# A re-laid first batch and a GpSimd broadcast for the second batch's softmax reciprocals, in a low-rank attention and gated FFN kernel

## The chip, the cores and the metric

One core of a Trainium2 chip runs the whole kernel. The metric is the device time of one execution, in microseconds (us), as the median of several; the span of a profiled execution is some 1.8 us shorter than its time. Runs of two kernels are compared when they alternate on the same chip.

## The reference, cut to what matters

```python
k_proj = np.einsum('ks,bhsd->bhkd', E, k)        # 8 batches, 8 heads, 1024 positions, 64 wide; k_proj has 64 rows
v_proj = np.einsum('ks,bhsd->bhkd', F, v)
scores = scale * np.matmul(q, k_proj.transpose(0, 1, 3, 2))
attn = np.exp(scores - max); attn = attn / (sum(attn) + 1e-09)
x = np.matmul(attn, v_proj)                      # then (8192, 512)
gate = 1.0 / (1.0 + np.exp(-(x @ w_gate)))       # w_gate, w_val: 512 x 1536
out = (gate * (x @ w_val)) @ w_out               # w_out: 1536 x 512
```

Nearly all the arithmetic is the FFN. Attention is a side chain of small steps, one batch ahead of it.

## The kernel before

The FFN of a batch is two blocks of 512 rows. A block is twelve m-steps (eight matmuls of 128x512, 1.73 us), four output projections of 2.7 us, and between them the next batch's attention is put at numbered places ("spots"). Batches, halves of a batch and blocks are counted from 0. Batch 0 has no FFN to hide behind: its first half is the start-up.

```python
# start-up (cut); busy(n) is n dummy matmuls of 128x128 that keep TensorE going
busy(40)
for R in range(2):                        # K, four heads at a time
    project(0, 0, [bk, bk], 0, R); busy(4); keep_k(bk, 0, R); turn_k(whole, R); busy(8)
qt(0, ("DVE", "ACT")); busy(6)            # Q transposed into one PSUM bank, copied out by two engines
sc(0); qt(1, ("DVE", "DVE")); busy(6)     # scores, exp
den(0); sc(1); busy(4)                    # row sums, reciprocal, split into two bf16 halves (rhi, rhl)
bc(0); den(1); v_part(0, whole); busy(4)  # broadcast of the reciprocals by matmuls; V
bc(1); xo(0); busy(8)                     # attention output, scaled: xT
v_part(1, att)
# ... the FFN's first pair of m-steps, with xo(1) between

# batch 1 (b == 1), one step per spot (cut)
def kv():  project K and V into one bank; keep_k; keep_v by four ScalarE copies
def den(): row sums of all eight heads, then four reciprocals of 128x128 on VectorE
def split(): two more VectorE instructions make rhl
def bc(rnd): four matmuls broadcast rhl, four ScalarE copies make rb
spots = (16, 17, 18, 19, 20, 20, 22, 23, 24, 25)   # kv, turn, sc, sc, den, split, bc, bc, xo, xo

# batches 2 to 7 in place of split and bc
def gather():  four SyncE DMAs of 8 KB bring one row per head into rrow
def spread(rnd): eight GpSimd broadcasts of 512 columns make rb
```

The softmax here doesn't subtract the row's maximum and nothing guards it: scores larger than these inputs give would overflow.

## Time and profile before

| | before |
|---|---|
| time, median of 3 at first | 576.91 us (576.17 to 576.95) |
| the execution of the profile | 575.25 us, span 573.4, mean clock 1.0 |
| TensorE busy | 97% of the span |
| first FFN matmul | 25.85 us |
| waits of TensorE in the first 93 us | 1.06, 0.93 and 1.02 in the start-up, 1.17 at block 1, 1.82 for rhl in batch 1 |

The row of the page that shows TensorE's busy share in 40 slices of 14.3 us, in tenths:

```profile
PE   5799989999999999999999999999999999999997
```

Apart from the last slice, all that is below 9 lies in the first six, so I looked at the first 90 us.

### The profile page before, as it was taken

To read this page: it belongs to the slowest core of one execution; us is meant where nothing else is said; L and a number is where in the kernel's file an instruction comes from. 1 tells how busy PE (TensorE), PEld (TensorE's weight loads), DVE (VectorE), ACT (ScalarE), POOL (GpSimd) and SP (SyncE) were. 2 spreads that over 40 slices of the span, in tenths; PEclk is the share of its full clock that TensorE was granted. 3 is DMA by queue.
4 is the path that set the end of the run, shared out by engine and by line. 5 is a ranking of instruction groups with operands and counts; after the bars stand their busy time and mean duration, and the time that the engine had idled before them with its cause. 6 is when DMAs were issued, how large, how long until landed. Compare 5 with 4: busy or idle time off the path is not lost.

```text
span 573.4 us, 7766 instructions
## 1 busy us (share of the span) xinstructions
PE 556.9 (97%) x3060; PEld 248.8 (43%) x3060; DVE 251.5 (44%) x403; ACT 176.2 (31%) x310; POOL 107.2 (19%) x148
## 2 busy tenths in 40 slices
PE   5799989999999999999999999999999999999997
PEld 5443434444444444444444444444444444444443
DVE  3546356325633546335453264434463354633332
ACT  2444561342224322333223422144223332222220
POOL 9400200104400071001800035000610007000000
PEclk9999999999999999999999999999999999999999
DMA  9999896955656159430796046670501101010012
GB/s 159 199 201 186 144 204 159 173 112 104 113 117 102 37 113 153 86 84 22 123 170 116 23 85 107 138 105 37 113 19 46 38 20 39 37 38 21 35 38 91
DMA packets 76421, 56.02 MB, mean 98 GB/s; under 512 B 34688, under 2 KB 67968, under 8 KB 76384
## 3 DMA queue, kind: packets, MB, share of 16 engines
q0 software_dynamic: 33984, 29.89, 34.4%
q1 hardware_dynamic: 42400, 25.63, 17.6%
q8 instruction: 24, 0.39, 0.3%
q14 instruction: 13, 0.11, 0.1%
HBM read 60.29 MB, written 16.78 MB: 134 GB/s over the span
## 4 chain that ended last, share of the span: by engine, by line
PE 95%; DVE 3%; ACT 1%; issue 0%; DVEq 0%
PE pF L210 86%; PE pA L210 9%; ACT eT L214 1%; DVE rden L769 1%; DVE xT L639 0%; DVE rden L583 0%; DVE count L327 0%; DVE hT L910 0%; DVE dsel L388 0%; ACT sig L214 0%; DVE rhl L780 0%; DVE rhl L594 0%; DVE ost L937 0%; ACT qT L214 0%; ACT kp L214 0%
## 5 line engine op out<-in xcount | busy, mean ns | idle before, releaser
L910 DVE SCALAR_TENSOR_TENSOR hT<-sig,pF 128x512 bf16<-128x512 f32 x192 | 130.7, 685 | 200.5 <-PE pF L210 153.1
L214 ACT ACTIVATE sig<-pF 128x512 f32<-128x512 f32 x192 | 114.3, 599 | 317.6 <-PE pF L210 315.2
L210 PE MATMUL pF<-xT,wG 128*128 128x512 bf16 x768 | 198.3, 379 | 1.8 <-DVE xT L639 1.8
L210 PE MATMUL pF<-xT,wV 128*128 128x512 bf16 x768 | 197.7, 379 | 0.0
L210 PE MATMUL pF<-wO,hT 128*128 128x512 bf16 x732 | 168.1, 379 | 0.0
L210 PEld LDWEIGHTS pF<-xT,wV 128*128 128x128 bf16 x768 | 75.2, 98 | 90.3
L210 PEld LDWEIGHTS pF<-xT,wG 128*128 128x128 bf16 x768 | 72.2, 98 | 96.6 <-issue 12.9
L815 POOL PARTITION_BROADCAST rb<-rrow x96 | 70.7, 798 | 217.1 <-DMA rrow<-rden 212.0
L210 PEld LDWEIGHTS pF<-wO,hT 128*128 128x128 bf16 x732 | 70.4, 98 | 88.7 <-issue 6.2
L937 DVE TENSOR_SCALAR ost<-pF 128x512 f32<-128x512 f32 x61 | 42.2, 692 | 97.8 <-PE pF L210 95.5
L214 ACT ACTIVATE eT<-pA 128x512 bf16<-128x512 f32 x62 | 32.2, 606 | 9.5 <-PE pA L210 9.5
L840 DVE TENSOR_TENSOR xT<-pA,rb 128x512 bf16<-128x512 f32 x56 | 34.7, 682 | 0.0
L228 POOL DMA_DIRECT2D KV<-in_v_dram x9 | 7.8, 871 | 87.3 <-PE pF L210 84.9
L769 DVE RECIPROCAL rden<-pA 128x128 f32<-128x128 f32 x28 | 23.7, 909 | 0.0
L210 PE MATMUL pA<-KV,EFT 128*64 128x512 bf16 (+2 forms) x176 | 15.4, 319 | 1.0 <-DVE xT L639 1.0
L214 ACT ACTIVATE kpd<-pA 64x1024 bf16<-64x1024 f32 x6 | 6.1, 1017 | 28.3 <-PE pA L210 28.3
L228 POOL DMA_DIRECT2D KV<-in_k_dram x9 | 8.0, 890 | 33.3 <-PE pF L210 33.2
L210 PEld LDWEIGHTS pA<-KV,EFT 128*64 128x64 bf16 x176 | 8.0, 109 | 8.0 <-issue 4.1
L210 PE MATMUL pA<-qT,kpD 64*64 64x512 bf16 (+1 forms) x136 | 10.2, 370 | 0.5 <-ACT qT L214 0.3
L210 PE MATMUL pA<-eT,vpD 64*64 64x512 bf16 (+1 forms) x140 | 10.4, 367 | 0.0
L214 ACT ACTIVATE vpD<-pA 64x512 bf16<-64x512 f32 (+2 forms) x20 | 9.7, 484 | 2.2 <-PE pA L210 1.8
L228 POOL DMA_DIRECT2D Qb<-in_q_dram x11 | 9.4, 866 | 0.0
(70 smaller groups left out, 109.3 us busy)
## 6 DMA issues: line engine op xcount, KB each, us to landing
out_dram<-ost SPq DMA_DIRECT2D x64, 256.0 KB, 2.0
Qb<-in_q_dram POOLq DMA_DIRECT2D x7, 1024.0 KB, 15.9
KV<-in_k_dram POOLq DMA_DIRECT2D x7, 1024.0 KB, 10.8
KV<-in_v_dram POOLq DMA_DIRECT2D x7, 1024.0 KB, 11.4
wO<-in_moe_w_out_dram POOLq DMA_DIRECT2D x1, 1536.0 KB, 13.0
wG<-in_moe_w_gate_dram POOLq DMA_DIRECT2D x5, 256.0 KB, 19.7
wV<-in_moe_w_val_dram POOLq DMA_DIRECT2D x5, 256.0 KB, 20.2
KV<-in_k_dram POOLq DMA_DIRECT2D x2, 512.0 KB, 8.9
```

The source lines that it names most:

```text
L210: return add("PE", lambda e: e.matmul(o, lhsT, rhs, **kw), r=r, x=[("bank", b)])
L214: return add("ACT", lambda e: e.activation(o, i, func, scale=scale), r=r, w=w, x=x)
L228: add("POOL", lambda e: e.dma_start(o, i), r=r, w=w, dma=sem)
L769: lambda e, cc=cc: e.reciprocal(rden[:, cc], bank[bk][:, cc]),
L815: lambda e, n=n, i=2 * rnd + c, j=j, parts=parts: e.partition_broadcast(rb[0:parts, n, :], rrow[32 * j : 32 * j + 1, i, :], channels=parts),
L840: lambda e, r=r, g=g, n=n, bk=bks[g]: e.tensor_tensor(xT[s][:, r, :, 256 * g : 256 * g + 256], bank[bk][:, :].rearrange("p (f c) -> p f c" ...
L910: lambda e: e.scalar_tensor_tensor(hT[blk % 2][:, m, :], sg[:, :], 1.0, bank[pv][:, :], ALU.add, ALU.mult,),
L937: lambda e: e.tensor_scalar(o[:, :], bank[pb][:, :], 0.5, None, op0=ALU.mult),
```

## The change

It has two parts. In batch 0 it drops dummies, gives each copy of the first Q half a bank of its own, puts the scores of the second half of heads ahead of the first half's row sums, and names every PSUM bank by hand. In batch 1 it projects K and V at different places, starts three m-steps earlier, and takes the reciprocals' way of the later batches: four gathers and sixteen GpSimd broadcasts in place of split, eight matmuls and eight ScalarE copies.

```diff
-        whole, ffn, att = Ring(AB + FB[:3]), Ring(FB), Ring(AB)
+        whole = Ring((A0, A1) + (A2, A3, F0, F1) + (A0, A1) + (F2, A2) + ...)   # cut, 26 turns by hand
+        ffn, att = Ring(FB), Ring(AB)
@@ qt: one bank per copy
-                bk = ring.next()
                 for rr, eng in enumerate(engines):
+                    bk = ring.next()
@@ start-up
-        busy(40)
+        busy(20)
...
-            busy(8)
+            busy(10 if R == 0 else 4)
...
+        sc(1)
         den(0)
-        sc(1)
-        busy(4)
+        busy(10)
+        den(1)
         bc(0)
-        den(1)
-        v_part(0, whole)
-        busy(4)
+        v_part(0)()
+        busy(6)
         bc(1)
         xo(0)
-        busy(8)
+        busy(4)
+        keep = v_part(1)
+        keep()
@@ batch 1
-                kv, turn_kd, sc(0), sc(1), den, split, bc(0), bc(1), xo(0), xo(1)          (cut)
-                spots = (16, 17, 18, 19, 20, 20, 22, 23, 24, 25)
+                k_alone, turn_k, v_alone, sc(0), sc(1), den, gather, spread(0), spread(1), xo(0), xo(1)
+                spots = (13, 14, 16, 16, 17, 18, 18, 18, 18, 24, 25)
```

The last four output projections also take their banks from another ring.

More of the change, by code (lines that the diff above doesn't have):

```diff
@@ L153, in bass_linformer_attn__then__ffn_glu_sigmoid_kernel @@
         dsel8 = sbuf("dsel8", [P, 2, 4, 32], BF16)
-        bsel = sbuf("bsel", [P, 2, 2, 64], BF16)
         bsel8 = sbuf("bsel8", [P, 4, 2, 64], BF16)
@@ L198, in next @@
                 return b
-        whole, ffn, att = Ring(AB + FB[:3]), Ring(FB), Ring(AB)
+        A0, A1, A2, A3 = AB
+        F0, F1, F2, F3 = FB
+        whole = Ring(
+            (A0, A1)
+            + (A2, A3, F0, F1)
+            + (A0, A1)
+            + (F2, A2)
+            + (A3, A3)
+            + (F0, F1)
+            + (A0, A1)
+            + (A2, A0)
+            + (A3, F0)
+            + (F1, F2)
+            + (A1, A2)
+            + (A3, A0)
+            + (A1, A2)
+        )
+        ffn, att = Ring(FB), Ring(AB)
         def mm(b, o, lhsT, rhs, r, start=True, stop=True, tp=None, tr=False):
@@ L398, in constants @@
                         )
-            for t, k, m, i, v in ((bsel8, "bsel8", 8, 1, 0.5), (bsel, "bsel", 4, 2, 0.25)):
+            for t, k, m, i, v in ((bsel8, "bsel8", 8, 1, 0.5),):
                 dve(
@@ L518, in qt @@
             def qt(R, engines):
-                bk = ring.next()
-                ob = bank[bk][:, :].bitcast(BF16)
-                for x in range(4):
-                    for t in range(2):
-                        c = x * 2 + t
-                        mm(
-                            bk,
-                            ob[:, c * P : (c + 1) * P],
-                            Qb[s][:, 4 * R + x, (2 * hf + t) * P : (2 * hf + t + 1) * P],
-                            ident[:, :],
-                            [("Q", s, hf, R), "ident"],
-                            tr=True,
-                        )
-                o = qv[:, R, :, 256 * hf : 256 * hf + 256]
-                i = ob[:, :].rearrange("p (x c) -> p x c", x=4)
-                for rr, eng in enumerate(engines):
-                    oo, ii = (a[:, 2 * rr : 2 * rr + 2, :] for a in (o, i))
+                for rr, eng in enumerate(engines):
+                    bk = ring.next()
+                    ob = bank[bk][:, :].bitcast(BF16)
+                    for x in range(2):
+                        for t in range(2):
+                            c = x * 2 + t
+                            mm(
+                                bk,
+                                ob[:, c * P : (c + 1) * P],
+                                Qb[s][:, 4 * R + 2 * rr + x, (2 * hf + t) * P : (2 * hf + t + 1) * P],
+                                ident[:, :],
+                                [("Q", s, hf, R), "ident"],
+                                tr=True,
+                            )
+                    o = qv[:, R, 2 * rr : 2 * rr + 2, 256 * hf : 256 * hf + 256]
+                    i = ob[:, 0:512].rearrange("p (x c) -> p x c", x=2)
                     ws = [("qT", s, hf, R, rr)]
                     if eng == "ACT":
-                        act(oo, ii, [], ws, b=bk)
+                        act(o, i, [], ws, b=bk)
                     else:
-                        dve(lambda e, oo=oo, ii=ii: e.tensor_copy(oo, ii), [], ws, b=bk)
+                        dve(lambda e, o=o, i=i: e.tensor_copy(o, i), [], ws, b=bk)
             def sc(R):
@@ L670, in kv @@
                 bk = att.next()
-                if b == 1:
-                    project(2 * b % 3, 0, [bk, bk], 0)
-                    project((2 * b + 1) % 3, 1, [bk, bk], 256)
-                    keep_k(bk, 0)
-                    keep_v([bk, bk], 256, ["ACT"] * 4)
-                    return
                 for t in range(NT):
@@ L708, in kv, with k_alone, v_alone @@
                     )
+            def k_alone():
+                bk = att.next()
+                project(2 * b % 3, 0, [bk, bk], 0)
+                keep_k(bk, 0)
+            def v_alone():
+                bk = att.next()
+                project((2 * b + 1) % 3, 1, [bk, bk], 0)
+                keep_v([bk, bk], 0, ["ACT"] * 4)
             def turn_kd():
-                if b == 1:
-                    turn_k(att)
-                    return
                 add(
@@ L773, in den @@
                     )
-            def split():
-                rd = [("rden", c, R) for c in range(4) for R in range(2)]
-                ri = [("rhi", R) for R in range(2)]
-                dve(lambda e: e.tensor_copy(rhi[:, :], rden[:, :]), rd, ri)
-                dve(
-                    lambda e: e.scalar_tensor_tensor(
-                        rhl[:, :], rhi[:, :], rows[:, 3, 0:1], rden[:, :], ALU.mult, ALU.add
-                    ),
-                    rd + ri + ["rows"],
-                    [("rhl", R) for R in range(2)],
-                )
-            def bc(rnd):
-                for j in range(4):
-                    n, bk, jj = 4 * rnd + j, att.next(), slice(32 * j, 32 * j + 32)
-                    mm(
-                        bk,
-                        bank[bk][:, :],
-                        bsel[jj, rnd, :, :].rearrange("p h d -> p (h d)"),
-                        rhl[jj, :],
-                        ["bsel", ("rhl", j // 2)],
-                        tp=(32 * j, 0),
-                    )
-                    act(rb[:, n, :], bank[bk][:, :], [], [("rb", n)], b=bk)
             def gather():
@@ L849, in xo @@
                         )
+            if b == 1:
+                return [
+                    k_alone,
+                    lambda: turn_k(att),
+                    v_alone,
+                    lambda: sc(0),
+                    lambda: sc(1),
+                    den,
+                    gather,
+                    lambda: spread(0),
+                    lambda: spread(1),
+                    lambda: xo(0),
+                    lambda: xo(1),
+                ]
             return [
@@ L856, in attention @@
                 den,
-                split if b == 1 else gather,
-                (lambda: bc(0)) if b == 1 else (lambda: spread(0)),
-                (lambda: bc(1)) if b == 1 else (lambda: spread(1)),
+                gather,
+                lambda: spread(0),
+                lambda: spread(1),
                 lambda: xo(0),
@@ L961, in bass_linformer_attn__then__ffn_glu_sigmoid_kernel, with v_part @@
             turn_k(whole, R)
-            busy(8)
+            busy(10 if R == 0 else 4)
+        def v_part(R):
+            bks = [whole.next(), whole.next()]
+            project(1, 1, bks, 0, R)
+            return lambda: keep_v(bks, 0, ["ACT", "DVE", "ACT", "DVE"], R)
         qt(0, ("DVE", "ACT"))
@@ L967, in bass_linformer_attn__then__ffn_glu_sigmoid_kernel @@
         busy(6)
+        sc(1)
         den(0)
-        sc(1)
-        busy(4)
-        def v_part(R, ring):
-            bks = [ring.next(), ring.next()]
-            project(1, 1, bks, 0, R)
-            keep_v(bks, 0, ["ACT", "DVE", "ACT", "DVE"], R)
+        busy(10)
+        den(1)
         bc(0)
-        den(1)
-        v_part(0, whole)
-        busy(4)
+        v_part(0)()
+        busy(6)
         bc(1)
         xo(0)
-        busy(8)
-        for _ in range(-att.turn % 4):
-            att.next()
-        v_part(1, att)
-        start_xo = half_unit(0, att)[4]
+        busy(4)
+        keep = v_part(1)
+        keep()
         load_q(1)
@@ L1018, in bass_linformer_attn__then__ffn_glu_sigmoid_kernel @@
                     if len(m) == 2:
-                        todo.append(lambda: first_pair(lambda: start_xo(1)))
+                        todo.append(lambda: first_pair(lambda: xo(1)))
                     else:
@@ L1030, in bass_linformer_attn__then__ffn_glu_sigmoid_kernel @@
             if b == 0:
-                qt, sc, den, bc, xo = half_unit(1, att)
-                put(5, lambda: (qt(0, ("DVE", "ACT")), qt(1, ("DVE", "ACT"))))
-                put(6, lambda: sc(0))
-                put(7, lambda: (den(0), sc(1)))
-                put(8, lambda: (den(1), bc(0)))
-                put(9, lambda: (xo(0), bc(1)))
-                put(10, lambda: xo(1))
-                spots = (16, 17, 18, 19, 20, 20, 22, 23, 24, 25)
+                qt2, sc2, den2, bc2, xo2 = half_unit(1, att)
+                put(5, lambda: (qt2(0, ("DVE", "ACT")), qt2(1, ("DVE", "ACT"))))
+                put(6, lambda: sc2(0))
+                put(7, lambda: (den2(0), sc2(1)))
+                put(8, lambda: (den2(1), bc2(0)))
+                put(9, lambda: (xo2(0), bc2(1)))
+                put(10, lambda: xo2(1))
+                spots = (13, 14, 16, 16, 17, 18, 18, 18, 18, 24, 25)
             else:
@@ L1062, in bass_linformer_attn__then__ffn_glu_sigmoid_kernel @@
         for tt in range(4):
-            oproj(last, tt, whole.next())
+            oproj(last, tt, ffn.next())
         plan.emit(nc, es, final=[f"out{i}" for i in range(4)])
```

## The prediction

> **What bounds the kernel now.** I read the page first (busy shares, then the chain that ended last), then TensorE in order of time with the idle time before each group, then the other engines around each gap, then the DMA issues with their time to landing. The page:
>
> ```profile
> PE 556.9 (97%) x3060; PEld 248.8 (43%) x3060; DVE 251.5 (44%) x403; ACT 176.2 (31%) x310; POOL 107.2 (19%) x148
> ...
> PE 95%; DVE 3%; ACT 1%; issue 0%; DVEq 0%
> ```
>
> TensorE is busy 97% of 573.4 us and carries 95% of the chain. A table of busy time by stretch gives TensorE 67.0 of the 67 us from 93 to 160, so what is saved before 93 us should pass to the end undiminished, and nothing else can pay. So only the first 93 us matter: start-up, one gap in batch 0, and the attention of batch 1 (batches, halves and blocks are counted from 0; a block's FFN is twelve m-steps of eight matmuls, 1.73 us each). TensorE in order of time (start, length, group, idle before it):
>
> ```profile
> 5.54 1.94 PE L210 MATMUL pA<-identf,EF 128*128 128x128 f32 x8 [5.54 <-DVE dsel L388]
> 7.28 3.76 PE L210 MATMUL pF<-ident 128*128 128x128 bf16 x40
> 10.97 0.64 PE L210 MATMUL pA<-KV,EFT 128*64 128x128 bf16 x16
> ...
> 20.11 0.22 PE L210 MATMUL pF<-rhl,bsel 32*128 32x128 bf16 x1 [1.06 <-DVE rhl L594]
> ...
> 25.28 0.64 PE L210 MATMUL pA<-KV,EFT 128*64 128x128 bf16 x16 [1.02 <-DVE xT L639]
> 25.85 0.39 PE L210 MATMUL pF<-xT,wG 128*128 128x512 bf16 x1
> ...
> 53.71 0.60 PE L210 MATMUL pF<-xT,wG 128*128 128x512 bf16 x2 [1.17 <-DVE xT L639]
> ...
> 80.46 0.40 PE L210 MATMUL pA<-rhl,bsel 32*128 32x512 bf16 x4 [1.82 <-DVE rhl L780]
> ```
>
> See the 40 dummy matmuls (pF<-ident) that only bridge to the first K data; the FFN's first matmul at 25.85; and the 1.82 us wait for the reciprocals' split in batch 1.
>
> **What the Trainium skill says.**
> - "TensorE: Matmul & The Clock Gate", Part 1, The HAM clock gate: the array runs at half clock until about 3.4 us of activity. The trace agrees: the 40 dummies start (3.76-0.22)/39 = 91 ns apart, eight later ones (0.62 us in all) 57 ns. With the page's 107 and 56 ns the switch is near 10.1 us, an estimate.
> - "Perfetto Trace Analysis", Matmuls: independent groups should rotate through PSUM banks so that eviction hides. The trace agrees: the Q transposes of one bank have two readers, and ScalarE idles 1.03 us before its copy, until VectorE's is done.
> - "DMA: Bandwidth & Descriptors", Queues, rings and completion order: a DMA engine alternates between its queues by packets, so a small transfer waits beside big loads. The trace agrees: an output store landed in 2.0 us at the median, in 4.8 when issued at 84.31, while loads ran.
> - "SBUF — State Buffer", Who interferes with whom: a VectorE instruction with one SBUF input doesn't contend with GpSimd outside its two-port modes. hT (one SBUF, one PSUM input) took 0.69 us during batch 2's broadcasts and before them.
>
> **Part 1, start-up.** The change drops 18 of 92 dummies, splits each Q-transposing bank, puts the scores of the second half of heads ahead of the first half's denominators, and lays banks out. Issue start plus time to landing gives the arrivals, which don't move: K halves 1.34+8.0 = 9.3 and 2.23+9.8 = 12.0; Q 13.4 and 14.7; V 18.4 and 20.9; first weights 21.5 to 23.7. Walking the new order with the old durations:
> - 20 dummies at 107 ns end near 9.5 instead of 11.0. K half 0 projects there, partly cold, done by 10.5. K half 1 then waits for data: 12.1 instead of 12.88, so 0.8 us saved, not 1.5.
> - The old chain from there to the transposed K is 1.36 us; four dummies instead of eight follow. Q transposes start near 13.7 (was 14.69). VectorE copies bank one from 14.05 (0.42) while ScalarE copies bank two from 14.3 (0.60), no longer in series. Scores end near 15.3 (was 16.75): 1.5 saved.
> - The second Q half puts both copies in one bank, so its second transposes wait for the first copy; its scores end near 17.2 (was 18.7). Denominators, 0.95+0.28+0.34 us of VectorE each, come 0.4 later behind the scores; the two chains run back to back on VectorE and end near 20.9 (was 22.6). V's two copies (0.62) end near 21.5, output matmuls start there (was 23.30), and xT lands 1.84 us later, near 23.4 (was 25.14).
> - V half 1 (landed 20.9) now projects while xT is written, where it used to cost 0.57 after it. FFN starts near 23.45.
>
> Saving 25.85-23.45 = **2.4 us**. Weights don't stop it: the tightest chunk, the fourth, lands at 33.0 (gate) and 34.3 (value), wanted at 37.45 and 38.32 less 2.4. The 1.17 us gap at 53.71 stays: its matmuls and VectorE chain are untouched.
>
> **Part 2, batch 1.** Other rows used:
>
> ```profile
> 66.03 1.57 ACT L214 ACTIVATE vpD<-pA 64x256 bf16<-64x256 f32 x4
> ...
> 75.77 3.38 DVE L769 RECIPROCAL rden<-pA 128x128 f32<-128x128 f32 x4
> 79.19 0.43 DVE L778 CAST rhi<-rden 128x512 bf16<-128x512 f32 x1
> 79.65 0.75 DVE L780 SCALAR_TENSOR_TENSOR rhl<-rhi,rows,rden 128x512 bf16<-128x512 bf16 x1
> ```
>
> GpSimd in batch 2, whose way batch 1 now takes (SyncE issued its four gathers from 133.29):
>
> ```profile
> 135.72 0.79 POOL L815 PARTITION_BROADCAST rb<-rrow  x1 [31.45 <-DMA rrow<-rden]
> 136.68 6.09 POOL L815 PARTITION_BROADCAST rb<-rrow  x8 [0.16 <-DVE ost L937]
> 142.93 5.43 POOL L815 PARTITION_BROADCAST rb<-rrow  x7 [0.16 <-POOL rb L815]
> ```
>
> Gone: eight broadcasting matmuls, two groups of 0.33 us, 0.66 on the path; the 1.82 us gap; eight ScalarE copies (4.1 us) and split's 1.2 us of VectorE, off the path. K and V matmuls stay at 32 (1.87 us). Gain 2.5 us. New costs on TensorE:
> - **V's bank.** V is projected directly before the scores. After K, its transpose and V, the scores' four banks end on V's own. V's four ScalarE copies take 1.57+0.1 us; TensorE has 0.35 us of score matmuls ahead of that bank. Wait 1.35 us.
> - **hT behind the reciprocals.** Four reciprocals (3.38 us) start about 0.9 after the denominators and delay the next hT to 5.0 after them. Four m-steps now follow without an output projection between; the third one's value matmuls want that hT's bank at 2.5x1.73 = 4.3. Wait 0.7 us.
> - **Broadcasts.** From first gather to the first eight broadcasts done is about 8.7 us, to all sixteen 15.1. Gathers start 4.3 us after the denominators, so rb is complete at 19.4 and the last xT 0.69 later, 20.1. TensorE's way from the denominators to block 2: four m-steps 6.92, the wait of 0.7, four projections 10.8, outputs 1.12, and 0.65 of block 2's own first matmuls, 20.2. With batch 2's latency it just fits; I count 0.05 us. But then the DMA engines were idle; here gathers go out near 74.5, when W_out and three 1 MB loads are under way (issued from 60.17, the last landing at 65.54+23.1 = 88.6). The store of 84.31, which met the same loads (the page's median is 2.0):
>
> ```profile
> out_dram<-ost SPq DMA_DIRECT2D x1, 256.0 KB, 4.8
> ```
>
> I add **1.3 us** for that, a choice between 0 and the store's extra 2.8, since only the first gathers hold the broadcasts up: the others land while GpSimd works.
>
> Sum by stage, from the block's start (53.28, the first m-step less its own gap) to block 2 (92.92), 39.64 us of old time: twelve m-steps 20.76, K and V 1.87, K's transpose 0.34, scores 1.16, denominators 0.6, broadcasting 0.66, outputs 1.12, four output projections 10.8, together 37.31; then the gap of 1.82 and some 0.5 of small idle between groups. New: 37.31-0.66+1.35+0.7+0.05+1.3 = 40.05 without the small idle, 40.55 with it: 0.4 to 0.9 us longer. I take +0.6. In other words the path through GpSimd gives back what the eight matmuls and their wait cost.
>
> **Total** -2.4+0.6 = -1.8 us: 576.9 becomes **575.1**. The last four output projections only change which banks they use; TensorE runs through them without a gap before, and each bank's last reader is done by the time, so nothing there.
>
> **Rivals.** (a) Batch 1 gains in full: V's bank or rb doesn't bite, total -2.4-2.5 = -4.9 us, 572.0. For it: all work removed was on the path. Against: the bank order is countable from the code. (b) Gathers crawl behind the loads and TensorE waits for rb: 2 to 3 us more, 577 to 578. For it: the store's 4.8 us, and Q transposes that took 13 us of SyncE at 44.7 but 5.4 at 91. Against: a gather is 8 KB, and only the first two delay the first broadcasts. (c) Start-up is hidden by data: K half 1 and V half 1 land where they land, saving 1 us only, 576.3. For it: 12.0 and 20.9 are close to when I use them. Against: the later gaps are VectorE's, not DMA's. (d) Fewer dummies leave the clock low for longer: +1 us; against it, TensorE stays busy until 9.5.
>
> **Range and chances.** Start-up -1.4 to -3.0, batch 1 -1.5 (part of rival a) to +2.5 (most of rival b), hardly both at one end: 573.2 to 577.0 holds eight in ten. 2% is 11.5 us, over twice what I can find in either direction.
>
> **What would show it.** First FFN matmul at 23 to 24 us with K half 1 at 12.1; ScalarE's Q copy no longer waiting for VectorE's; in batch 1 a TensorE wait of about 1.3 us for vpD inside the scores, one of 0.7 for hT, none for rhl, and one for xT (through rb) at block 2; the span moved by as much as block 2's start. A first FFN matmul later than 25, or xT waits over 3 us, would make it wrong.

## More of the kernel before

The time of this kernel depends on the clock that TensorE is granted, and the mean of that clock is on record for each execution.

The profiled execution was 1.66 us faster than the median of the timed ones.

## The result, and the profile after

| | before | after |
|---|---|---|
| time, median of 4 | 576.91 us | 577.25 us (576.25 to 578.26) |
| ratio | | 1.0009, 95% interval 0.9987 to 1.0031: the same |
| span of the profiled execution (clock 1.0 both) | 573.4 | 574.8 |
| first FFN matmul on record | 25.85 (gate), 26.08 (value) | 24.34 (value; the gate's record is missing) |
| first value matmul of block 2 | 93.78 | 95.20 |

A ratio is the mean time of one kernel's fast runs over that of the other's fast runs of the same rounds, so it isn't quite the ratio of the medians.

The start-up came in 1.74 us earlier (26.08 to 24.34) and block 2 began 1.42 us later. So between the two, batch 1 lost 3.16 us. From block 2 on nothing changes: the span is longer by the same 1.4. The page after, busy shares and the chain that ended last:

```profile
PE 552.6 (96%) x2979; PEld 247.4 (43%) x3034; DVE 250.9 (44%) x400; ACT 172.6 (30%) x302; POOL 118.8 (21%) x164
...
PE 92%; POOL 2%; DVE 2%; DMA 2%; issue 1%; ACT 0%; SPq 0%; POOLq 0%; DVEq 0%
```

GpSimd (POOL) and DMA had no share of the chain before; now each has 2%. Of DMA's two, by the page's shares by line, one is the gathers (rrow<-rden) and the other the load of a constant at the start. TensorE in order of time, as in the prediction:

```profile
9.56 1.06 PE L226 MATMUL pA<-KV,EFT 128*64 128x128 bf16 x16
...
12.10 0.64 PE L226 MATMUL pF<-KV,EFT 128*64 128x128 bf16 x16
...
66.33 0.41 PE L226 MATMUL pA<-qT,kpD 64*64 64x512 bf16 x3 [1.16 <-ACT vpD L230]
...
76.18 1.04 PE L226 MATMUL pF<-xT,wV 128*128 128x512 bf16 x4 [0.25 <-DVE hT L915]
...
88.72 0.40 PE L226 MATMUL pA<-eT,vpD 64*64 64x512 bf16 x2 [0.79 <-DVE xT L831]
...
94.98 0.39 PE L226 MATMUL pF<-xT,wG 128*128 128x512 bf16 x1 [2.52 <-DVE xT L831]
```

The two K halves start at 9.56 and 12.10, as walked. The wait for rhl at 80 us is gone. In its place stand four: for V's bank, for hT behind the reciprocals, and two for xT. The last two add up to 3.31 us, and VectorE, which the view names, is not to blame for them. The chain in order of time (here the second of the four gathers), and GpSimd's first broadcast of batch 1, say what VectorE waited for:

```profile
76.28 5.18 DMA rrow<-rden
```

```profile
81.54 0.79 POOL L806 PARTITION_BROADCAST rb<-rrow  x1 [18.24 <-DMA rrow<-rden]
```

The first gather was issued at 75.61, and the first broadcast started 5.93 us later. In batch 2 of the kernel before the same distance is 135.72-133.29 = 2.43.

One line explains part of the start-up's shortfall, the first conversion of the reciprocals to bf16 on VectorE:

```profile
18.84 0.61 DVE L604 CAST rhi<-rden 64x128 bf16<-64x128 f32 x1
```

It took 0.27 us before. GpSimd was issuing the K and V loads of batch 1 from 18.34 to 20.27, beside it. But it was doing so beside the 0.27 us of the kernel before too, so why this one is longer stays open.

### The profile page after: what moved, and what is told of

Its sections match the earlier page's. It is cut to its first block, busy times and chain, and to the rows that moved or that the text cites. A ratio compares the mean times of both kernels' runs of the same rounds, so it can differ in the third digit from the quotient of the medians.

```text
span 574.8 us, 7675 instructions
## 1 busy us (share of the span) xinstructions
PE 552.6 (96%) x2979; PEld 247.4 (43%) x3034; DVE 250.9 (44%) x400; ACT 172.6 (30%) x302; POOL 118.8 (21%) x164
## 4 chain that ended last, share of the span: by engine, by line
PE 92%; POOL 2%; DVE 2%; DMA 2%; issue 1%; ACT 0%; SPq 0%; POOLq 0%; DVEq 0%
PE pF L226 85%; PE pA L226 7%; POOL rb L806 2%; DMA rrow<-rden 1%; DMA EF<-in_F_dram 1%; DVE xT L654 0%; DVE rden L598 0%; ACT vpD L230 0%; DVE hT L915 0%; DVE rhi L604 0%; DVE vpD L501 0%; DVE xT L831 0%; DVE rhl L609 0%; DVE ost L942 0%; ACT qT L230 0%
## 5 line engine op out<-in xcount | busy, mean ns | idle before, releaser
L226 PE MATMUL pF<-xT,wG 128*128 128x512 bf16 x748 | 194.9, 379 | 5.9 <-DVE xT L831 2.5
L226 PE MATMUL pF<-wO,hT 128*128 128x512 bf16 x750 | 173.9, 379 | 1.4 <-issue 0.6
L806 POOL PARTITION_BROADCAST rb<-rrow x112 | 82.6, 798 | 236.2 <-DMA rrow<-rden 230.2
L226 PEld LDWEIGHTS pF<-wO,hT 128*128 128x128 bf16 x768 | 73.9, 98 | 93.0 <-issue 5.6
L942 DVE TENSOR_SCALAR ost<-pF 128x512 f32<-128x512 f32 x64 | 44.2, 691 | 102.4 <-PE pF L226 102.4
```

Of the source, the lines that this page charges most:

```text
L226: return add("PE", lambda e: e.matmul(o, lhsT, rhs, **kw), r=r, x=[("bank", b)])
L806: lambda e, n=n, i=2 * rnd + c, j=j, parts=parts: e.partition_broadcast(rb[0:parts, n, :], rrow[32 * j : 32 * j + 1, i, :], channels=parts),
L942: lambda e: e.tensor_scalar(o[:, :], bank[pb][:, :], 0.5, None, op0=ALU.mult),
```

## The experiments

All twelve runs gave correct results. The theory: the start-up pays some 1.7 us, and batch 1 gives back more, because the gathers collide with batch 2's loads on the DMA engines. The rivals: the collision is only there because the start moved; GpSimd or the gather is slow by itself. A third, the clock, came up with the first results.

### Each part alone

`e1_start_only`: the new batch 0, the old batch 1.

```diff
-                k_alone, turn_k, v_alone, ... gather, spread(0), spread(1), ...
-                spots = (13, 14, 16, 16, 17, 18, 18, 18, 18, 24, 25)
+                kv, turn_kd, ... split, bc(0), bc(1), ...
+                spots = (16, 17, 18, 19, 20, 20, 22, 23, 24, 25)
```

> The new first batch alone; batch 1 keeps its broadcasting matmuls and its old places. Theory (the parts add up: start-up saves 1.7 us, as the first FFN matmuls of the changed kernel show, and batch 1 loses 3.2): faster than before by 1.7 us, a span near 571.7 where before has 573.4 with the same clock, and batch 1's wait for the split of the reciprocals stays 1.8 us. Rival (the earlier start is eaten later whatever batch 1 does, by data or by the clock): within 0.5 us of before.

Measured: 573.72 us (572.96 to 573.73) against 576.90, ratio 0.994 (0.9923 to 0.9957). The span is 571.9, 1.5 below the trace of before, as expected; the wait for rhl is still there:

```profile
78.95 0.40 PE L227 MATMUL pA<-rhl,bsel 32*128 32x512 bf16 x4 [1.82 <-DVE rhl L796]
```

But the median gained 3.2 us, twice what the traces differ by. The clock means tell why: all six runs of this kernel stand at 0.999 or 1.0, and of the eleven runs of before beside it only two do (575.29 and 575.36). Six stand at 0.993 or 0.994 (576.05 to 577.33), three at 0.991 (578.01 to 578.20).

`e2_batch1_only`: the old batch 0, the new batch 1 (the same edit the other way round).

> The new batch 1 alone, old first batch. Theory: slower than before by 3.1 us (span near 576.5): a wait of 1.2 us for V's bank inside the scores, 0.3 to 0.4 for hT, and 3.3 together for xT, because the gathers take over 5 us to land while the loads run. Rival (the gathers collide with the loads only because the new start brings them 1.7 us forward): gathers land in under 4 us here and the loss is under 1.5 us.

Measured: 581.17 us (577.49 to 581.95), ratio 1.0065 (1.0037 to 1.0093): more than the theory's loss. The waits are as expected where they were named (1.16 for V's bank, 0.25 for hT, 2.51 for xT at block 2), though there is none on the view inside the output matmuls. The first gather was issued at 78.79 and the first broadcast started at 84.02: 5.2 us, so the rival that needs the earlier start falls. (The distance varies: the changed kernel's batch 1 has 5.93 in one trace and 81.51-75.61 = 5.90 in another, `after_again`, and 80.83-75.61 = 5.22 in e8.) What I hadn't counted is the clock. Five of its six runs have a mean of 0.988 to 0.991, and the table of stretches shows where the clock was halved (length, busy times of the engines, then PEclk, DMA share and GB/s as the last three columns):

```profile
22.70:29.50 6.80, 5.71 (x52) 2.78 (x48) 2.76 (x7) 1.62 (x4) 0.00 (x0) 0.50 1.45 197
...
97.80:101.10 3.30, 3.30 (x10) 1.13 (x8) 0.88 (x2) 0.60 (x1) 0.57 (x1) 0.50 0.63 155
```

PEclk is 0.50 in both, 1.00 in the stretches between. The first lies at the end of the old start-up, the second right behind the wait for xT that ended at 97.45. The one run with the clock at 1.0 took 577.49, 2.2 us over before's 575.30 at that clock (the mean of nine such runs), so without the clock the loss of this part was nearer 2 than 3 us.

### Two of the named waits

`e3_v_earlier`: V one m-step ahead of the scores.

```diff
-                spots = (13, 14, 16, 16, 17, 18, 18, 18, 18, 24, 25)
+                spots = (13, 14, 15, 16, 17, 18, 18, 18, 18, 24, 25)
```

> The changed kernel with V projected one m-step earlier, so that its four evictions lie under that m-step. Theory (V's bank costs 1.16 us on TensorE and everything behind shifts with it, gathers included): that wait gone, span 1.2 us less, 573.6; the waits for xT at block 2 unchanged at 3.3. Rival (the loads decide when the gathers land, not the time they are issued): the wait goes but the xT waits grow to 4.5, span unchanged at 574.8.

Measured: 575.44 us (574.68 to 576.16), ratio 0.9975 (0.9957 to 0.9993). The wait for V's bank is gone, and the broadcasts started 2.1 us earlier, at 79.41 for 81.54. The wait for xT at block 2 is still 2.52. The span, 574.4, looks like no gain, but this execution had its clock halved right behind that wait. Two lines of TensorE show it:

```profile
92.83 0.39 PE L226 MATMUL pF<-xT,wG 128*128 128x512 bf16 x1 [2.52 <-DVE xT L831]
...
94.31 1.92 PE L226 MATMUL pF<-xT,wG 128*128 128x512 bf16 x4
```

Block 2's awaited matmul came at 92.83 instead of 94.98. Four gate matmuls that take 1.03 us at full clock then took 1.92. So 2.15 us came where 1.2 were expected. The chain to it: the first gather was issued 1.39 us earlier (74.22 for 75.61), and the first broadcast followed 5.19 us after it, not 5.93. The second step is the size by which this distance varies anyway. Of the six runs four are at clock 1.0.

`e4_loads_after`: the Q and V loads of batch 2 wait for the reciprocals, beside the gathers; W_out and K stay ahead.

```diff
-                put(17, lambda: load_next(2))
+                put(17, lambda: load_k(2))
@@ batch 1
-                    gather,
+                    lambda: (gather(), load_rest()),     # load_q(2), load_v(2), both after the reciprocals
```

> The changed kernel with the Q and V loads of batch 2 issued only when the reciprocals are done, just beside the gathers, instead of 14 us ahead; W_out and K stay. Theory (the gathers are slow because they share the DMA engines with those loads): the first broadcast starts 2.4 to 3.5 us after the first gather's issue instead of 5.9, the xT waits drop from 3.3 to about 0.5, span near 572. Rival (the first broadcast is late for another reason, GpSimd itself or the gather's own path): the first broadcast still 5.9 us after the gather, and the span no better, or worse if V comes too late for batch 2's projection.

Measured: 574.49 us (574.43 to 575.34), ratio 0.9961 (0.9944 to 0.9978), span 572.9. The direction is right and the size is a miss: the first broadcast came 4.0 us after the gather, not 2.4 to 3.5; the wait inside the output matmuls vanished, but the one at block 2 fell only to 1.79. The chain in this kernel:

```profile
76.28 3.26 DMA rrow<-rden
```

The Q and V loads were issued at 76.04 and 76.91, right among the gathers.

`e9_loads_last`: Q and V behind the first eight broadcasts (shown against e4).

```diff
-                    lambda: (gather(), load_rest()),
-                    lambda: spread(0),
+                    gather,
+                    lambda: (spread(0), load_rest()),
```

> The changed kernel with only the Q and V loads of batch 2 moved behind the first eight broadcasts; W_out and K stay ahead (K lands near 76.5, after the gathers' issue at 75.6). The held loads of before still left 4.0 us from gather to broadcast. Theory (what is left is the end of K's load plus the starting Q and V loads): about 3 us from the first gather's issue to the first broadcast. Rival (K's end alone sets it): still 4.0. Batch 2's projection may wait for V here, which is not the question.

Measured: one run, 576.32 us. From first gather (75.64) to first broadcast (78.08) 2.44 us. In the chain:

```profile
76.31 1.68 DMA rrow<-rden
```

`e10_all_loads_last`: K's load moved there too.

> The same with K's load moved there too, so that after W_out's landing near 72 the DMA engines are idle when the gathers go out. Theory (5.9 us from gather to broadcast is sharing with loads and nothing else): 2.4 to 2.6 us, as in the later batches, and the first TensorE wait for xT inside the output matmuls gone. Rival (the first use of the gather or the broadcast costs time of its own): over 3.5. K and V come late for batch 2, so the span will be several us longer; it is a measurement of the gather only.

Measured: one run, 582.45 us (it starves batch 2, as said; V is waited for 3.75 us), and 78.93-76.51 = 2.42 us to the first broadcast. The expectation that the wait for xT inside the output matmuls would go held. So the gathers are as fast as in later batches once Q and V are out of the way; between these two looks the end of K's load makes no difference. The gather landed 5.2 us after its issue with the loads queued ahead, 3.3 with them starting beside it, 1.7 with Q and V held back. It is not GpSimd. The price of this order is also in the traces: between the eighth and the ninth broadcast GpSimd issues the loads, for 1.80 us in e9 (84.48 to 86.28) and 2.67 in e10 (85.16 to 87.83), and the wait for xT at block 2 is 2.15 and 2.71. An estimate: without this issue some 0.4 us of wait would be left in e9 and none in e10, near the 0.05 that the prediction had for gathers that meet no loads. In e9 V also comes 0.68 us late.

How the loads hold a gather up isn't shown. In e4's trace the DMA engines are 4% busy from 76 to 77 us, while the second gather is under way and the two loads are only being issued; so the collision need not be one for the engines' time.

### The clock

`e7_before_filled`: the kernel before, with dummies where TensorE stood still.

```diff
-        sc(1); busy(4)
+        sc(1); busy(20)
-        v_part(0, whole); busy(4)
+        v_part(0, whole); busy(18)
-        xo(0); busy(8)
+        xo(0); busy(24)
```

> The kernel before with more dummy matmuls in the three places of its first batch where TensorE stands still for about a microsecond (4 to 20, 4 to 18, 8 to 24), none on the path. Theory (in most runs of the kernel before, TensorE's clock is halved for some 6.8 us because it does too little between 18 and 26 us; nine of its eleven runs show a mean clock of 0.991 to 0.994): nearly all runs at clock 1.0, median about 575.3, 1.6 us faster than before, though nothing on the path got shorter. Rival (the halved windows come from elsewhere, or the clock means are noise of the record): the same spread of clocks and 576.9.

Measured: 575.24 us (574.43 to 576.12) against 576.27, ratio 0.9978 (0.9959 to 0.9997); all six runs at 0.999 or 1.0, where the eleven beside it had three. The span is 573.4, exactly that of the trace of before: the traced execution got no shorter, and the executions at a lower clock are gone. The clock isn't all that spreads the times: at full clock two of the six took 576.11 and 576.12, the others 574.43 to 575.25. What the dummies changed is TensorE's busy time from 18.4 to 25.9 us, first in the kernel before, then filled:

```profile
18.40:25.90 7.50, 4.27 (x89) 2.85 (x90) 4.90 (x10) 3.67 (x8) 2.10 (x3) 1.00 1.44 196
```

```profile
18.40:25.90 7.50, 6.86 (x135) 5.44 (x136) 4.87 (x10) 3.67 (x8) 2.09 (x3) 1.00 1.45 196
```

`e8_after_filled`: the changed kernel, 44 dummies in front of the matmul that waits at block 2.

```diff
                 for i in range(NI):
+                    if (blk, m, n, i) == (2, 0, "G", 3):
+                        fill(44)
                     mm_one(blk, m, i, n, pbs[n])
```

> The changed kernel with 44 dummy matmuls in front of the matmul of block 2 that waits 2.5 us for the last xT. Theory (that wait halves the clock for one window of 3.4 us in about half the runs, which costs 1.7 us again): all runs at clock 1.0, median near 576.4, spread under 0.8 us. Rival (the half-clock window has another cause): runs at 0.997 and times of 577.9 to 578.3 stay.

Measured: 576.47 us (575.94 to 577.35), ratio 1.0 (0.9982 to 1.0018). Five of six at 1.0, and one still at 0.997 (577.35), so not all, and the spread is 1.4 us and not under 0.8. With four of ten for the changed kernel itself this is too few to be shown by counting.

`after_again` and `before_again`: both kernels unchanged.

> The changed kernel unchanged, for the count of its clock states. Theory: two states, about half of the runs at clock 1.0 with 576.2 to 576.7 us, the others at 0.997 with 577.8 to 578.3; the runs of before beside it at 1.0 (575.3), 0.994 (576.1 to 576.9) and 0.991 (578.0). At clock 1.0 the change loses about 1.1 us. Rival: the states don't go with the times.

> The kernel before unchanged, for a trace of an execution with a halved clock (eight of eleven runs had one). Theory: the halved windows lie in the first batch, between about 20 and 32 us, where TensorE stands still three times for a microsecond; the span is then 1 to 1.6 us longer than the 573.4 of the trace that I predicted from. Rival: they lie at block 2 or elsewhere.

Measured: `after_again` 576.61 us (576.12 to 578.64), ratio 1.001 (0.9991 to 1.003). With the first four the changed kernel has ten runs: six at clock 1.0, 576.12 to 576.68, mean 576.41; four at 0.997, 577.39 to 578.64, mean 578.04. The states go with the times. `before_again` was a miss: the one look fell at clock 1.0 (575.31 us), so I have no trace of the kernel before itself with a halved clock. That it is halved near 23 to 30 us there rests on the same first batch in e2's trace and on e7.

### What beats both

`e5_both`: e3 and e4 together.

> The changed kernel with V an m-step earlier and the Q and V loads held until the reciprocals. Theory (the two costs are separate): span 572.9 of the held loads less 1.2 to 1.4, near 571.6, time near 573.4, all runs at clock 1.0 because the xT wait shrinks below 1 us. Rival: gathers issued 1.2 us earlier meet W_out and K still loading (K lands at 76.5) and gain nothing: wait for xT 1.8 or more, span near 572.5.

Measured: 572.71 us (572.52 to 573.28), ratio 0.9936 (0.9918 to 0.9953), span 570.9. The gain is the expected one and more, but the wait for xT stayed at 1.93 us and not below 1: the gathers still met the starting loads, 77.64-73.49 = 4.15 us. 0.7 us of the gain is the start-up of this execution, whose first FFN matmul came at 23.41 for 24.13 in e8: its clock is on record as full from 8.7 us on, e8's from 11.0.

`e6_early_matmul`: the new start-up, K and V apart and early, but the reciprocals broadcast by matmuls.

```diff
-                k_alone, turn_k, v_alone, sc(0), sc(1), den, gather, spread(0), spread(1), xo(0), xo(1)
-                spots = (13, 14, 16, 16, 17, 18, 18, 18, 18, 24, 25)
+                k_alone, turn_k, v_alone, sc(0), sc(1), den, split, bc(0), bc(1), xo(0), xo(1)
+                spots = (13, 14, 15, 16, 17, 18, 20, 22, 23, 24, 25)
```

> New first batch; batch 1 with K and V projected apart, at 13 and 15, scores at 16 and 17, denominators at 18 as in the changed kernel with V earlier, but the reciprocals split and broadcast by the old matmuls at 22 and 23. Theory (the old wait of 1.82 us came from the late denominators, not from the matmul way, and GpSimd's way costs 3.3 us of waits): no wait for rhl over 0.1 us, 0.3 for hT, none for xT; span 1.4 us under the start-up-alone kernel, near 570.5, time near 572.3, the fastest of all. Rival (split's 1.2 us of VectorE and the eight ScalarE copies now collide with the gates of four m-steps in a row): hT waits grow to 1.5 and the gain over the start-up alone is under 0.5.

Measured: 572.20 us (571.81 to 572.51), ratio 0.9923 (0.9904 to 0.9943): the fastest of all, 0.8% under before. All six runs at 0.999 or 1.0. In batch 1 TensorE has one wait left that the view shows between 60 and 90 us:

```profile
75.04 1.04 PE L227 MATMUL pF<-xT,wV 128*128 128x512 bf16 x4 [0.25 <-DVE hT L950]
```

The wait of 1.82 us that the change set out to remove came from starting batch 1's attention late, not from the matmuls: they cost 0.66 us of TensorE, and the way through GpSimd cost 3.31 us of waits.

## Why the prediction was wrong

The range ended at 577.0 and the first median was 577.25. By its own steps:

- **Where to look** held: everything that changed lies before block 2, and the span followed block 2's start to 0.1 us.
- **Start-up, 2.4 us: right in kind, 0.7 too large.** 1.7 came. K half 0 at 9.56, K half 1 at 12.10 and scores done at 15.3 were as walked. The shortfall starts at the row sums, whose first reciprocal began at 17.86 where the walk has about 17.6, and at the conversion behind it, sized 0.28 and measured at 0.61; the two chains run back to back, so both delays, 0.6 us together, pass on.
- **V's bank, 1.35, and hT, 0.7:** both there, 1.16 and 0.25 on the view. e3 shows that the first was on the path.
- **The gathers: the step that failed.** "I add 1.3 us for that" is the term that was mis-sized. Gather to broadcast took 5.93 us for 2.43, 3.5 more, and the TensorE waits for xT were 3.31 us where the sum has 0.05+1.3. My argument for a small number, that a gather is only 8 KB and only the first ones count, took size as the measure. The runs show that what counts here is which loads are under way (5.2, 3.3 and 1.7 us to land, in the changed kernel, e4 and e9). "DMA: Bandwidth & Descriptors" in the Trainium skill, which the prediction cites, states only that queues take turns by packets; that a small transfer waits was my inference, and how long it waits is what I got wrong. The store that I had before me, 2.8 us longer beside the same loads, was the better guide, and I took less than half of it. This was rival (b), whose 577 to 578 is what came.
- **The total was set on the wrong floor.** I took the walk from an execution at full clock (575.25) and subtracted from a median of executions most of which had a halved clock for a while (of 33 runs of before, nine at full clock with a mean of 575.30, 24 slower). From 575.25 the same steps would have said 573.4. At full clock the changed kernel takes 576.41, so the steps are 3 us short together: 0.7 in the start-up, the rest in batch 1 (sized +0.6, measured +3.16 in the trace). The +0.6 was itself low: with the small idle on both sides the prediction's own sum is 40.55 against 39.64, +0.9; it took a value between a sum with that idle and one without. That 575.1 came within 2.2 us of the median is partly luck.
- **Rival (d) had the sign wrong.** Fewer dummies at the start did not leave the clock low: the new start-up, in e1, e5 and e6, has no run of eighteen under 0.999. It does the opposite, and is worth 3.2 us in medians where the traces show 1.5. e7 shows that filled pauses keep the clock; that the new start-up keeps it for the same reason is likely and not shown, for its pauses are fewer but hardly shorter (0.90 and 0.89 us on the changed kernel's view, where before has 1.06, 0.93 and 1.02). The changed kernel can lose the clock elsewhere, four runs in ten at 0.997, I think at block 2, though none of its own traces caught it. In three traces (e2, e3, e10) the half clock begins within 0.7 us behind a wait of 2.5 us or more; that the wait is its cause is likely and not shown: e8's count is too small, and both traces of the changed kernel (2.52 and 2.51 us) and e10's (2.71) have this wait at block 2 with a full clock behind it.

Why the change gained nothing, then: 1.7 us of start-up at full clock are saved and 2.5 us of work and waits in batch 1 are removed, and new waits of 4.7 us (1.16, 0.25, 3.31) are bought with them; 4.7 less 2.5 leaves 0.9 of the 3.16 us that batch 1 lost, in smaller delays that I can't name one by one (by the prediction's own sum its "small idle between groups" grew from some 0.5 to 1.4 us).

## What to carry to other kernels

A hand-off over DMA can be small and still slow: here one gather of 8 KB took 1.7 to 5.2 us to land, by what loads were under way beside it. Before moving a hand-off onto DMA, look what loads run at that moment and take the time to landing from a transfer that met such loads. A wait at a late step may come from a chain that started late; moving the chain's start, as e6 does, was worth more than replacing its last link. And compare the time of the profiled execution with the median of the timed ones before subtracting from either.

## What the Trainium skill lacked or had wrong

- "TensorE: Matmul & The Clock Gate" advises against idle gaps over about 3 us. Here shorter pauses were followed by half clock: 6.8 us of it at the end of the old start-up (e2's trace; the same stretch of before has no pause over 1.1 us, and TensorE busy 4.27 of 7.5 us), gone in six of six runs when the pauses are filled (e7); and 3.4 us behind a wait of 2.52 us (e3's trace). In e2's trace itself the longest pause before the first of these windows is 1.33 us. The page does say, for a kernel that rotates PSUM banks, that frequent short idles throttle the clock again, but gives no length for them. The lengths of the half clock, 3.4 us and twice that, agree with the page's window.
- "DMA: Bandwidth & Descriptors" describes how queues take turns but has no figure for a small transfer beside large ones. The second of four gathers of 8 KB landed after 5.2 us with 1 MB loads queued, 3.3 with two of them starting, 1.7 with these two held back.
- "SBUF — State Buffer" says that two-port VectorE instructions contend with GpSimd; it speaks of a VectorE measurement 6.8 times slower, but not of which instruction, and has no figure for a conversion beside load issues. The first 64x128 conversion from f32 to bf16 took 0.47 to 0.66 us in six traces (the changed kernel, e1 to e5) where GpSimd was issuing loads beside it, and up to 0.82 in others, the second, after those issues, 0.22 or 0.23 in five of them. In three traces with the old start-up (before, before_again, e7) the first took 0.22 to 0.27 in spite of such an issue beside it. I did not isolate it.
- No page that I read has the cost of the GpSimd broadcast: 0.80 us for 512 columns of f32, 12.6 us for the sixteen of a batch.
- No page warns that the profiled execution can be in another clock state than most timed ones: 575.25 against a median of 576.91 us.
